# The end of an attention and maxout kernel: general-path transfers on GpSimd's queue, a last chunk of 384 and 128 columns, and a VectorE copy

## The chip, the cores and the metric

The kernel runs on one core of a Trainium2 chip. The metric is the device time of one execution in microseconds (us); a set of runs is given by its median. The profile is of one execution, and its times count from the first instruction of the program. Engines are TensorE (PE; PEld its weight loads), VectorE (DVE), ScalarE (ACT), GpSimd (POOL) and SyncE (SP). SyncE computes nothing here: it issues the DMA transfers and waits.

## The reference

For each of 8 batches and 8 heads, 512 tokens of width 64 attend to 32 state rows and the state rows attend to the tokens. The 512 + 32 rows of a batch, all heads side by side (512 columns), then pass a maxout layer.

```python
scores = scale * np.matmul(x, state.transpose(0, 1, 3, 2))     # softmax over the state rows
xread = np.matmul(a, state)
scores2 = scale * np.matmul(state, x.transpose(0, 1, 3, 2))    # softmax over the tokens
sread = np.matmul(a2, x)
x = concat([xread, sread], axis=2)  ->  (B * 544, 512)
h1 = x @ w1; h2 = x @ w2
out = np.maximum(h1, h2) @ w_out                               # float32, 4352 x 512
```

Softmax subtracts the maximum of each row first.

## The kernel before

The softmax is computed without subtracting a maximum, and the result is right as long as no sum of exponentials leaves a wide range. A flag is set where one does. Everything is computed by this fast path; then comes `tc.If(left_range >= 1, label="general")` at L658, whose body computes all batches again with the maximum subtracted. With the inputs here the flag is zero, the body is skipped, and every engine jumps over its own part of it. TensorE and ScalarE are given a hint at L631 that this jump is likely; VectorE, GpSimd and SyncE are not.

Maxout is rewritten as relu(x(w1 - w2)) w_out + x(w2 w_out). In the kernel `wd` is w1 - w2, `wo` is w_out and `wwo` is w2 w_out. For each batch, `SW[b]` holds the state times those two weights, `AT[b]` the transposed softmax weights, and `R[b]` the relu. `l1` computes `R`, and `l2(b, c)` computes a chunk `c` of 128 token rows by 512 columns: `l2_open` (2 matmuls at L384) opens the sum in a bank of the matmul memory, `l2_f` (8 matmuls at L389) adds the relu part, `l2_out` copies the bank into the batch's output tile `OB[b]`, and `store` (L405) sends it off. The state rows of all batches are done once at the end: `m1` (L418) and `m2(t)` (L426, L428), whose result goes out in four transfers of 64 KB each (L432). `copy` runs on ScalarE (L99), VectorE (L101) or GpSimd (L103).

Batches 0 and 1 run by an order written out by hand (`ORDER`), batches 2 to 6 in a loop, and batch 7 in a section of its own (L621 to L649). There the order is: `l1` of all 8 blocks, `m1`, the hints, the flag read into a register of every engine (L635), chunk 0 and both `m2` copied by VectorE, chunks 1 and 2 copied by ScalarE, and chunk 3 in two halves of 256 columns, each with its own bank, copied by ScalarE and stored by SyncE as soon as it is copied. The trailing copy at L653 waits for the store of chunk 2 to land, and a one-element matmul (L655) waits for that copy.

All transfers are issued from SyncE's queue, in program order, those of the general path too: two loads of `x` for each batch (L151), one store for each batch (L405) and eight of the state rows (L432). Completion is counted on eight DMA semaphores, taken in turn. For an engine or a semaphore that the general path would advance, the path that skips it has instructions that wait for the count so far and add what the body would have added (L658 in the profile). After that come closing waits on SyncE for every DMA semaphore and every engine's count, then a meeting of all engines, a clear of the program's semaphores by GpSimd, and a second meeting (all L740).

Of the kernel before, what the change touches and what calls it, by code (L numbers as in the profile page):

```python
# [48 lines left out]
def kernel(  # L49
# [9 lines left out]
    nc = tc.nc  # L59
    B, H, S, D = x.shape  # L60
    _, _, Ns, _ = state.shape
    L = S + Ns
# [25 lines left out]
    def bank(ring="r", dtype=F32):  # L88
        if isinstance(ring, int):
            i = ring  # L90
        else:
            r = rings[ring]
            i = r[turn[ring] % len(r)]
            turn[ring] += 1
        return banks[i] if dtype == F32 else banks[i].bitcast(BF16)

    def copy(eng, o, i):
        if eng == "A":
            nc.scalar.copy(o, i)  # L99
        elif eng == "V":  # L100
            nc.vector.tensor_copy(o, i)  # L101
        else:
            nc.gpsimd.tensor_copy(o, i)  # L103
# [36 lines left out]
    def h8(*shape):  # L140
        return stage.tile([128, *shape], F32, tag="h8", bufs=10, name="h8")
# [3 lines left out]
            wh[w, h] = h8(4, 512)  # L145
        return wh[w, h]

    def load_x(b, g):
        if b not in xf_t:
            xf_t[b] = h8(H, NC * D)  # L150
        nc.sync.dma_start(  # L151
            out=xf_t[b][:, 4 * g:4 * g + 4, :],
            in_=x[b, 4 * g:4 * g + 4].rearrange("h (p c) d -> p h (c d)", c=NC),
        )
# [53 lines left out]
    def d_(b):  # L208
        return st.setdefault(b, {})

    def cast_e(b, k, eng):
        d = d_(b)
        d["xe"] = xe[of_xe[b]]
        copy(eng, d["xe"][:, :, k, 8:136].rearrange("p c (j d) -> p j c d", j=2),
             xf_t[b][:, 2 * k:2 * k + 2, :].rearrange("p j (c d) -> p j c d", c=NC))
# [87 lines left out]
    def sr_mm(b, ring, nb=1):  # L303
        p = bank(ring)
        for j in range(nb):
            d = d_(b + j)
            for c in range(NC):
                for g in range(2):
                    for k in range(4):
                        o = 130 * j + 65 * g  # L310
                        nc.tensor.matmul(p[32 * k:32 * k + 32, o:o + 65], d["e"][:, g, c, k],  # L311
                                         d["xe"][:, c, k, 7 + 65 * g:72 + 65 * g],
                                         start=(j == 0 and c == 0 and g == 0),
                                         stop=(j == nb - 1 and c == NC - 1 and g == 1), skip_group_check=True)
        return p
# [9 lines left out]
    def sr_tr(b, ring, nb=1):  # L325
        p = bank(ring, BF16)
        for j in range(nb):
            nc.tensor.transpose(p[:, 128 * j:128 * j + 128], d_(b)["sr"][:, j].rearrange("p g d -> p (g d)"), ident)
        return p
# [52 lines left out]
    def l2_open(b, c, p, start, stop, lo=0, hi=DM):  # L382
        for g in range(2):
            nc.tensor.matmul(p[:, lo:hi], AT[b][:, g, c, :], SW[b][:, g, FF + lo:FF + hi],  # L384
                             start=(start and g == 0), stop=(stop and g == 1))

    def l2_f(b, c, p, fs, start, stop, lo=0, hi=DM):
        for j, f in enumerate(fs):
            nc.tensor.matmul(p[:, lo:hi], R[b][:, f, c * 128:(c + 1) * 128], wo[:, f, lo:hi],  # L389
                             start=(start and j == 0), stop=(stop and j == len(fs) - 1))  # L390

    def l2_out(b, c, p, eng, lo=0, hi=DM):
        if b not in OB:
            OB[b] = h8(NC, DM)
        copy(eng, OB[b][:, c, lo:hi], p[:, lo:hi])
# [7 lines left out]
    def store(b, c0=0, c1=NC, lo=0, hi=DM, eng=None):  # L403
        dst = out[b * L:b * L + S].rearrange("(p c) n -> p c n", c=NC)
        (eng or nc.sync).dma_start(out=dst[:, c0:c1, lo:hi], in_=OB[b][:, c0:c1, lo:hi])  # L405


    RS = {}
# [10 lines left out]
                                          start=(i == 0), stop=(i == 3))  # L419
        relu(RS["r"][:, f, :], p[:, 0:NT], eng)  # L420

    def m2(t, eng):
        p = bank("a")
        ts = slice(t * 128, (t + 1) * 128)
        for i in range(4):
            nc.tensor.matmul(p, sread_t[:, i, ts], wwo[:, i, :], start=(i == 0), stop=False)  # L426
        for f in range(NF):
            nc.tensor.matmul(p, RS["r"][:, f, ts], wo[:, f, :], start=False, stop=(f == NF - 1))  # L428
        copy(eng, RS["o"][:, t, :], p)
        for q in range(4):  # L430
            b = 4 * t + q
            nc.sync.dma_start(out=out[b * L + S:(b + 1) * L], in_=RS["o"][32 * q:32 * q + 32, t, :])  # L432


    def w2_cast(f, n, eng):
# [108 lines left out]
    for tok in toks:  # L544
        name, _, eng = tok.partition(">")
# [10 lines left out]
        elif w in mms:  # L556
            ring = [int(v) for v in ring]
            p = mms[w](*n, ring if w == "sw" else ring[0] if ring else None)
# [7 lines left out]
    for b in range(2, B - 1):  # L566
# [23 lines left out]
        if n in reads:  # L590
            p = sr_mm(*reads[n][:1], "a", reads[n][1])
# [18 lines left out]
        if n in reads:  # L610
            p = sr_tr(reads[n][0], "r", reads[n][1])
            sr_cp(p, reads[n][0], "A", reads[n][1])
        if n == B - 1:
            p = bank("r")
# [6 lines left out]
    b = B - 1  # L621
# [19 lines left out]
    store(b, 1, 2)  # L641
    l2(b, 2, "A")
    store(b, 2, 3)
    for lo, hi in ((0, 256), (256, 512)):
        p = bank("a")
        l2_open(b, 3, p, True, False, lo, hi)
        l2_f(b, 3, p, range(NF), False, True, lo, hi)
        l2_out(b, 3, p, "A", lo, hi)
        store(b, 3, 4, lo, hi)  # L649


# [2 lines left out]
    p = bank("a")  # L654
# [3 lines left out]
    with tc.If(left_range >= 1, label="general"):  # L658
        of_xe, of_e = [0, 1] * 4, [0, 1] * 4
        xf_t.clear(), st.clear(), AT.clear(), SW.clear(), R.clear(), OB.clear()  # L660
        mx = at.tile([128, 2 * NC, 2], F32, tag="mx", bufs=1, name="mx")
        cm = at.tile([64, 2], F32, tag="cm", bufs=1, name="cm")
        dl = h8(NC, DM)[:, 0, :]
        e2 = at.tile([64, 512], BF16, tag="e2", bufs=1, name="e2")
        for b in range(B):
            d = d_(b)
            for g in range(2):
                load_x(b, g)
            for k in range(4):
                cast_e(b, k, "PV"[k % 2])  # L670
            for hh in range(2):
                xt_ev(xt_mm(b, 2 * hh, 2, "r"), b, 2 * hh, 2, "V")
            for hh in range(2):
                pv = sc_mm(b, 2 * hh, 2).rearrange("p (c g i n) -> p g c i n", c=NC, g=2, i=2)
                for g in range(2):
                    m = mx[:, 4 * g:4 * g + 4]
                    dv = dl[:, 256 * g:256 * g + 256].rearrange("p (c i n) -> p c i n", c=NC, i=2)
                    nc.vector.tensor_reduce(m, pv[:, g], axis=AXX, op=ALU.max)
                    nc.vector.tensor_tensor(dv, pv[:, g], m.unsqueeze(3).to_broadcast([128, NC, 2, Ns]),
                                            op=ALU.subtract)  # L680
                nc.scalar.activation(out=e_view(b, 2 * hh, 2), in_=dl.rearrange("p (m i n) -> p m i n", i=2, n=Ns),
                                     func=ACTF.Exp, scale=scale)
                norm_sum(b, 2 * hh, 2)
                norm_mul(b, 2 * hh, 2, "V")
            for g in range(2):
                at_ev(at_mm(b, g, "r"), b, g, "V")
            for k in range(4):
                p = bank("r")
                for c in range(NC):
                    nc.tensor.matmul(p[0:64, c * 128:(c + 1) * 128], sbd[:, b, k, :], d["xt"][:, c, k, :],  # L690
                                     start=(c == 0), stop=(c == NC - 1))
                nc.vector.tensor_reduce(cm[:, 0:1], p[0:64], axis=AXX, op=ALU.max)
                nc.vector.tensor_scalar(cm[:, 1:2], cm[:, 0:1], scalar1=-scale, scalar2=None, op0=ALU.mult)
                nc.scalar.activation(out=e2, in_=p[0:64], func=ACTF.Exp, bias=cm[:, 1:2], scale=scale)
                pt = bank("r", BF16)
                for c in range(NC):
                    nc.tensor.transpose(pt[:, c * 64:(c + 1) * 64], e2[:, c * 128:(c + 1) * 128], ident[0:64, 0:64])
                copy("V", d["e"][:, :, :, k, :], pt[:, 0:256].rearrange("p (c g n) -> p g c n", c=NC, g=2))
            sr_ev(sr_mm(b, "r"), b)
            sr_cp(sr_tr(b, "r"), b, "V")  # L700
            for z in range(3):
                p = sw_mm(b, 512 * z, 512 * z + 512)
                for g in range(2):
                    sw_ev(p, b, 512 * z, 512 * z + 512, g, "V")
            for f in range(NF):
                l1(b, f, "V")
            for c in range(NC):
                l2(b, c, "V")
            store(b)
        m_open()  # L710
        for f in range(NF):
            m1(f, "V")
        for t in range(NT // 128):
            m2(t, "V")


# [28 lines left out]
```

## Time and profile before

| | |
|---|---|
| three runs | median 149.26 us, 148.87 to 149.98 |
| the profiled execution | 149.64 us, span from first to last instruction 147.8 us |
| mean granted TensorE clock | 0.994 |
| busy in the span | PE 140.6, DVE 79.6, ACT 67.7, POOL 52.9 us |
| DMA | 29.08 MB, mean 197 GB/s |

The span is what the page and the trace divide up; 1.8 us of the profiled execution lie around it. A busy TensorE is a matmul in flight, and matmuls overlap, so its share counts occupation. In the rows of groups the columns are the line, the engine, the operation, output and inputs, the shapes, the count, then busy time in us and the mean of one in ns, then the idle time ahead of them and what ended most of it. A row of one source line in the trace gives an engine (q for its instruction sequencer), the operation, the count, shortest/median/longest duration in ns, and the first and last start in us.

### The profile page before, as it was taken

Reading aid. Unit: us, or ns where it says so; the run is one execution under the profiler, and the core shown is the slowest. Engines: PE = TensorE matmul, PEld = TensorE weight load, DVE = VectorE, ACT = ScalarE, POOL = GpSimd, SP = SyncE. Lnnn points to the kernel's source line nnn. Section 1 sums busy time; section 2 is a strip of 40 time slices with the busy share of each in tenths; the row PEclk is TensorE's granted clock in tenths of the full one; section 3 lists DMA queues with packets and bytes.
Section 4 is the critical chain, followed back from the end, with each engine's and each line's share of the span. In section 5 each row is a group of like instructions: output and inputs, shape, how many; then the busy total and the mean of one; then the engine's idle time right before and its main releaser. Section 6 shows DMA issues by size and latency. Waiting matters only on the chain.

```text
span 147.8 us, 3126 instructions
## 1 busy us (share of the span) xinstructions
PE 140.6 (95%) x1254; PEld 68.8 (47%) x1254; DVE 79.6 (54%) x148; ACT 67.7 (46%) x130; POOL 52.9 (36%) x81
## 2 busy tenths in 40 slices
PE   6968999999999999999999999999999999999990
PEld 2534455445444445454534443454545344754460
DVE  3367754867599048463854575274637476632100
ACT  4367572677894236225632735270447145510121
POOL 3174315356996050924192447228300500000000
PEclk9999999999999999999999999999999999999997
DMA  4899999995786769495949698796306072002452
GB/s 146 249 379 361 363 362 246 338 349 190 137 301 133 186 231 305 88 263 191 279 80 306 246 124 158 266 315 115 75 29 255 0 212 112 35 0 82 104 180 78
DMA packets 35374, 29.08 MB, mean 197 GB/s; under 512 B 19900, under 2 KB 32444, under 8 KB 34588
## 3 DMA queue, kind: packets, MB, share of 16 engines
q1 hardware_dynamic: 35356, 28.84, 66.8%
q8 instruction: 11, 0.18, 0.5%
q14 instruction: 7, 0.06, 0.2%
HBM read 15.20 MB, written 8.91 MB: 163 GB/s over the span
## 4 chain that ended last, share of the span: by engine, by line
PE 70%; SPq 14%; DMA 10%; POOL 3%; issue 1%; ACT 1%; ACTq 0%
PE bank L389 32%; PE bank L371 16%; DMA h<-in_x_dram 8%; PE bank L384 8%; SPq L159 5%; SPq L163 4%; PE bank L344 4%; SPq L151 3%; PE bank L418 2%; PE bank L428 2%; PE bank L259 2%; PE bank L311 2%; SPq L192 2%; DMA out_dram<-h 1%; POOL xb L103 1%; PE bank L426 1%
## 5 line engine op out<-in xcount | busy, mean ns | idle before, releaser
L389 PE MATMUL bank<-wo,r 128*128 128x512 bf16 (+1 forms) x232 | 53.1, 372 | 0.0
L99 ACT COPY h<-bank 128x512 f32<-128x512 f32 (+1 forms) x20 | 11.1, 566 | 53.5 <-PE bank L389 49.0
L389 PEld LDWEIGHTS <-r 128*128 128x128 bf16 x232 | 22.7, 98 | 25.7
L371 PE MATMUL bank<-aT,sw 128*128 128x512 bf16 x128 | 29.8, 379 | 0.0
L362 DVE TENSOR_SCALAR r<-bank 128x512 bf16<-128x512 f32 x30 | 20.5, 690 | 13.9 <-PE bank L371 13.6
L360 ACT ACTIVATE r<-bank 128x512 bf16<-128x512 f32 x34 | 20.1, 598 | 7.4 <-PE bank L371 7.3
L277 POOL TENSOR_TENSOR a<-e,er 128x512 bf16<-128x512 bf16 (+1 forms) x13 | 12.3, 964 | 20.6 <-ACT e L267 16.4
L101 DVE CAST sw<-bank 128x512 bf16<-128x512 f32 (+1 forms) x23 | 13.7, 636 | 9.5 <-PE bank L344 9.4
L103 POOL CAST xb<-h 128x1024 bf16<-128x1024 f32 x12 | 12.4, 1039 | 17.6 <-issue 16.5
L371 PEld LDWEIGHTS <-sw 128*128 128x128 bf16 x128 | 12.0, 98 | 13.2 <-issue 0.2
L103 POOL CAST xe<-h 128x512 bf16<-128x512 f32 x24 | 14.4, 632 | 7.6 <-DMA h<-in_x_dram 7.6
L384 PE MATMUL bank<-sw,aT 128*128 128x512 bf16 (+1 forms) x58 | 16.9, 373 | 0.0
L99 ACT CAST sw<-bank 128x512 bf16<-128x512 f32 (+1 forms) x29 | 14.8, 572 | 1.6 <-PE bank L344 1.6
L101 DVE COPY h<-bank 128x512 f32<-128x512 f32 x13 | 8.7, 670 | 11.4 <-PE bank L389 11.3
L273 DVE TENSOR_REDUCE sums<-e 128x16 f32<-128x512 bf16 (+1 forms) x14 | 8.2, 586 | 1.7 <-ACT e L267 1.4
L463 PE MATMUL bank<-wo,w2t 128*128 128x512 bf16 x32 | 8.1, 379 | 0.5 <-ACT w2t L99 0.5
L516 PE MATMUL bank<-wo,r 128*128 128x512 bf16 x32 | 8.1, 379 | 0.0
L452 DVE TENSOR_TENSOR wd<-h,h 128x512 bf16<-128x512 f32 x7 | 5.8, 858 | 3.0 <-DMA h<-in_moe_w_dram 3.0
L471 PE MATMUL bank<-wz 128*128 128x512 bf16 x15 | 6.2, 565 | 1.2 <-DVE wz L474 1.2
L384 PEld LDWEIGHTS <-aT 128*128 128x128 bf16 x58 | 4.8, 98 | 5.2 <-issue 1.3
L267 ACT ACTIVATE e<-bank 128x512 bf16<-128x512 f32 (+1 forms) x14 | 6.8, 533 | 0.9 <-PE bank L259 0.4
L259 PEld LDWEIGHTS <-xt 128*128 128x128 bf16 x128 | 5.0, 98 | 2.6 <-DVE xt L101 0.6
(86 smaller groups left out, 122.8 us busy)
## 6 DMA issues: line engine op xcount, KB each, us to landing
h<-in_x_dram SPq DMA_DIRECT2D x16, 512.0 KB, 5.8
out_dram<-h SPq DMA_DIRECT2D x6, 1024.0 KB, 4.3
h<-in_moe_w_dram SPq DMA_DIRECT2D x8, 512.0 KB, 9.2
h<-in_moe_w_out_dram SPq DMA_DIRECT2D x4, 512.0 KB, 9.1
out_dram<-h SPq DMA_DIRECT2D x2, 512.0 KB, 3.7
out_dram<-h SPq DMA_DIRECT2D x3, 256.0 KB, 2.2
out_dram<-rs SPq DMA_DIRECT2D x8, 64.0 KB, 2.3
sf<-in_state_dram SPq DMA_DIRECT2D x2, 224.0 KB
```

The lines of the kernel that those rows point to most:

```text
L99: nc.scalar.copy(o, i)
L101: nc.vector.tensor_copy(o, i)
L103: nc.gpsimd.tensor_copy(o, i)
L273: nc.vector.tensor_reduce(s_, e_view(b, k0, kn), axis=AXX, op=ALU.add)
L277: (nc.gpsimd if eng == "P" else nc.vector).tensor_mul(e_view(b, k0, kn, "a"), e_view(b, k0, kn), d_(b)["er"][:, :, k0:k0 + kn].unsqueeze(3 ...
L360: recent["A"] = nc.scalar.activation(out=o, in_=p, func=ACTF.Relu)
L362: nc.vector.tensor_scalar(o, p, scalar1=0.0, scalar2=None, op0=ALU.max)
L371: nc.tensor.matmul(p, SW[b][:, g, f * 128:(f + 1) * 128], AT[b][:, g].rearrange("p c t -> p (c t)"), start=(g == 0), stop=(g == 1))
L384: nc.tensor.matmul(p[:, lo:hi], AT[b][:, g, c, :], SW[b][:, g, FF + lo:FF + hi], start=(start and g == 0), stop=(stop and g == 1))
L389: nc.tensor.matmul(p[:, lo:hi], R[b][:, f, c * 128:(c + 1) * 128], wo[:, f, lo:hi], start=(start and j == 0), stop=(stop and j == len(fs) ...
L463: nc.tensor.matmul(ACC[key], w2t[:, j, i, :], wo[:, j, :], start=first(key), stop=last(key, j == f + n - 1))
L516: nc.tensor.matmul(p, R[b][:, j, c * 128:(c + 1) * 128], wo[:, j, :], start=first(key), stop=last(key, j == f + n - 1))
```

## The change

Three edits. `load_x` and `m2` take an engine to issue from, and the general path passes `nc.gpsimd` to them and to `store`. So all 32 transfers of the general path move from SyncE's queue to GpSimd's; the fast path's transfers stay where they are. The last chunk of batch 7 is split at column 384 in place of 256, and its second part, now 128 columns, is copied by VectorE; ScalarE copies the first.

```diff
-    def load_x(b, g):
+    def load_x(b, g, eng=None):
         if b not in xf_t:
             xf_t[b] = h8(H, NC * D)
-        nc.sync.dma_start(
+        (eng or nc.sync).dma_start(
...
-    def m2(t, eng):
+    def m2(t, eng, dma=None):
...
-            nc.sync.dma_start(out=out[b * L + S:(b + 1) * L], in_=RS["o"][32 * q:32 * q + 32, t, :])
+            (dma or nc.sync).dma_start(out=out[b * L + S:(b + 1) * L], in_=RS["o"][32 * q:32 * q + 32, t, :])
...
-    for lo, hi in ((0, 256), (256, 512)):
+    for lo, hi, eng in ((0, 384, "A"), (384, 512, "V")):
         p = bank("a")
         l2_open(b, 3, p, True, False, lo, hi)
         l2_f(b, 3, p, range(NF), False, True, lo, hi)
-        l2_out(b, 3, p, "A", lo, hi)
+        l2_out(b, 3, p, eng, lo, hi)
         store(b, 3, 4, lo, hi)
...
             for g in range(2):
-                load_x(b, g)
+                load_x(b, g, nc.gpsimd)
...
-            store(b)
+            store(b, eng=nc.gpsimd)
...
         for t in range(NT // 128):
-            m2(t, "V")
+            m2(t, "V", nc.gpsimd)
```

In the program this makes, the order on each engine is the same up to the last chunk. TensorE then has ten matmuls of 384 and ten of 128 columns where it had twenty of 256; ScalarE has one copy fewer and VectorE one more, directly ahead of its branch at L658. In the part that skips the general path, SyncE's eight instructions on DMA semaphores are gone, and GpSimd has four waits and one instruction for eight new semaphores of its own queue. SyncE's closing waits are twelve instead of eight, each naming up to two semaphores: the four first name the new ones, the next eight are the old ones, in the old order and with the same engine counts beside them.

## The prediction

> **What bounds the kernel now.** I read the page's busy times and its chain of waits first.
>
> ```profile
> PE 140.6 (95%) x1254; PEld 68.8 (47%) x1254; DVE 79.6 (54%) x148; ACT 67.7 (46%) x130; POOL 52.9 (36%) x81
> ...
> PE 70%; SPq 14%; DMA 10%; POOL 3%; issue 1%; ACT 1%; ACTq 0%
> ```
>
> TensorE bounds the body: 140.6 us of a 147.8 us span, and most of the chain. The change leaves the body alone. The order of the instructions shows no difference on any engine before the last chunk of batch 7, so everything up to 141.7 us should stand. What can move are the 6 us from there to the span's end, so next I read the timeline of the end.
>
> ```profile
> 141.75 0.38 PE L384 MATMUL bank<-sw,aT 128*128 128x256 bf16 x2
> ...
> 143.04 0.37 ACT L99 COPY h<-bank 128x256 f32<-128x256 f32 x1 [0.51 <-PE bank L389]
> 143.06 1.04 PE L389 MATMUL bank<-wo,r 128*128 128x256 bf16 x8
> 144.13 0.37 ACT L99 COPY h<-bank 128x256 f32<-128x256 f32 x1 [0.72 <-PE bank L389]
> 144.68 0.19 ACT L653 CAST h<-wz 128x1 f32<-128x1 bf16 x1 [0.17 <-DMA out_dram<-h]
> 144.92 0.09 PEld L655 LDWEIGHTS bank<-h 128*1 128x1 f32 x2 [1.11 <-ACT h L653]
> ```
>
> The last matmul's result is free at 144.11, ScalarE copies it until 144.50, SyncE issues the last store at 144.53 and it lands at 146.44 (the last two are from the trace's DMA records). No engine computes after 145.2, and yet the span runs to 147.83. Third, therefore, the branch around the general path (L658) and the closing waits (L740), SyncE's in the stretch behind 146 us.
>
> ```profile
> L658 SPq EVENT_SEMAPHORE  x8: 17/17/17, 145.1 to 146.5; - x8
> L658 POOLq COMPARE_BRANCH  x1: 45/45/45, 124.1 to 124.1; - x1
> L658 POOLq EVENT_SEMAPHORE  x1: 17/17/17, 124.3 to 124.3; - x1
> L658 DVEq COMPARE_BRANCH  x1: 72/72/72, 137.7 to 137.7; - x1
> L658 DVEq EVENT_SEMAPHORE  x1: 21/21/21, 140.8 to 140.8; - x1
> L658 ACTq COMPARE_BRANCH  x1: 68/68/68, 144.7 to 144.7; - x1
> L658 SPq COMPARE_BRANCH  x1: 45/45/45, 144.9 to 144.9; - x1
> ```
> ```profile
> L740 SPq EVENT_SEMAPHORE  x8: 28/28/28, 146.5 to 147.0; - x8
> L740 SPq DRAIN  x2: 7/10/13, 147.0 to 147.1; - x2
> ```
>
> Two things are to be seen. (a) SyncE, on the path that skips the general block, makes up for that block's DMAs: eight instructions that wait for one DMA semaphore each and add to it. Seven are through by 145.6; the eighth waits for the last landing and goes at 146.46. Only then come eight more waits (L740), 62 ns apart, then two drains and the meeting of all engines: 146.46 to 147.83 is 1.37 us. (b) From VectorE's branch to its next instruction 3.08 us pass (137.72 to 140.80), against 0.18 to 0.19 on GpSimd (124.09 to 124.27) and SyncE (144.91 to 145.10). The copy before that branch was done at 138.39, so it explains at most 0.7 of the 3.08. VectorE's part of the general path is some 430 instructions long and that jump has no prefetch hint; TensorE's and ScalarE's have one (L631). Now this stall costs nothing: VectorE is through by 140.9, six microseconds early.
>
> **The change, part by part.**
>
> *SyncE's part of the general path.* Its 32 DMAs go to GpSimd's program. In the program that the change makes, SyncE's skip block is empty, and its closing waits are twelve: four for the GpSimd queue's new semaphores, then the old eight, each of them asking for less. All but the last can pass before the last store lands. What lay behind the landing, 146.46 to 147.10 (second drain), shrinks to the last wait and two drains: from the last L740 wait at 146.965 to the end are 0.87 us where the landing had 1.37. Worth -0.50, provided that SyncE waits for nothing else.
>
> *GpSimd.* Its skip block gains four waits on semaphores that ask for zero and one instruction that adds to the eight new semaphores. It takes its branch at 124.1, 23 us before it is needed; by the row of the same instruction at the span's start (27 ns) and GpSimd's closing steps of under 0.2 us this is about 0.5 us, or 3.6 if its longer block made it stall as VectorE does. Nothing in either case. If that cover were gone, it would be 0.5 to 3.6 on the end. The 32 transfers themselves are not executed, since the flag is zero.
>
> *The closing clear* takes 25 semaphores instead of 17. The row has 135 ns for 17; between no change and in proportion (+64 ns) I take +0.03.
>
> *384 and 128 columns.* TensorE issues ten matmuls of 512 columns every 216 ns and of 256 every 109 ns, which makes 0.416 ns a column and 2.6 ns apiece (64-column ones at L259 come every 29 ns, as this has it). Ten of 384 and ten of 128 give 10 x (162.5 + 55.9) = 2.18 us, as before: the end of TensorE stays at 144.11. The 384 columns are free at about 143.55 instead of 143.02. ScalarE's copy of them costs 0.48 (a 128x384 copy took 485 ns), to 144.05 (a wait that it gets ahead of it asks for a VectorE copy done at 133.1), and its store is issued at 144.08 instead of 143.44.
>
> *The last 128 columns on VectorE.* It has been idle since 138.4 and its copy is not queued behind anything. Rows near it: 420 ns for 256 columns, 682 for 512, hence 290 for 128 (an operation on 128x128 from the same memory took 291). 144.13 to 144.42, where ScalarE ended at 144.50. But SyncE is in the issue of the 384 columns until 144.41, and 0.09 lies between one issue and the next (143.77 to 143.81, then 47 ns as at 140.47): the last store goes at 144.51 instead of 144.53. It is 64 KB behind 192 KB, where now 128 KB follow 128 KB. Landing after issue was 1.92 for the last one; 64 KB stores of L432 show 1.6 to 3.4, median 2.3. I take 1.92, as the nearest in place: 146.42, bounds 146.1 to 146.8 (by 2.3). So by this route alone the end would come at 146.42 + 0.02 + 0.87 = 147.3, which is -0.53, +0.03 for the clear.
>
> *The branch behind that copy.* A step that the words of the change don't name, and the one that decides. VectorE's branch is in order behind its last copy. That was dispatched at 137.70, with the branch 23 ns later; now it is dispatched at 144.13, the branch at 144.15. With the 3.08 us of its own row, its next instruction, which adds to VectorE's semaphore, comes at 147.23 and is seen at 147.26. Queued behind it is VectorE's drain for the meeting (0.12 later); and SyncE waits for it, because its closing wait for the third-last store asks for VectorE's full count too. SyncE arrives there at about 145.7 and stands until 147.28. It passed the same wait at 146.844, and 0.99 us follow (two waits, two drains, the meeting, the clear). The landing at 146.4 is hidden under this.
>
> *Sum.* 147.28 - 146.84 = +0.43, +0.03 for the clear: +0.46 us. On the profiled execution: span 147.83 to 148.29, time 149.64 to 150.10 (1.81 lie around the span). That execution is 0.38 over the median of the three runs, 149.26, so I forecast 149.26 + 0.46 = 149.7.
>
> [...]
>
> Bounds of the stall: instruction-queue packets of 8 KB took 0.31 to 0.84 us, the one nearest behind VectorE's branch (138.75) 0.54. With the shortest the stall is 2.85, with the longest 3.4, and if another engine's packet (0.55 at 145.76) goes ahead of it, 3.9. Together 149.5 to 150.5 for this case.
>
> **The rivals.**
>
> *Faster: VectorE's stall is short in its new place.* If VectorE idles for six microseconds ahead of the branch, and something fetches its target meanwhile, it costs what SyncE's does (0.19), VectorE is through by 144.5, and the last store binds: 149.26 - 0.53 + 0.03 = 148.8. It turns at a stall of 3.08 - 0.46 = 2.62 us: under this the change is faster. For it: ScalarE's branch cost 0.48 with a hint long before it, so an early fetch works. Against it: VectorE was idle ahead of its branch before as well (1.97 us before the copy at 137.70), and still took 3.08. [...]
>
> *Longer stall.* The last stores (145.2 to 145.9) and the pages that SyncE, ScalarE and TensorE fetch when they branch (144.7 to 144.9) now share the queues with VectorE's fetch. One page of 1.3 us as at 146.06 ahead of it: 149.7 + 1.3 = 151.0. Against it: the stretch 137.7 to 140.8 was no lighter, the DMA engines busy 39% of it, against 30% in 144.1 to 147.2.
>
> *The GpSimd queue costs something outside the skip block.* A program that uses this queue may need more around the span, where 1.81 us lie now; doubled, 149.7 + 1.8 = 151.5. Nothing in the order of the instructions shows it: the start is the same in both, down to an instruction on that queue's semaphores at 0.14 us.
>
> **How the numbers follow.** A measurement of this kernel tells about 1%, 1.5 us, from no change. Forecast 0.60 (0.57 within 1%, 0.03 slower); faster rival 0.20 (0.16 within, 0.04 faster, should the landing come early as well); longer stall 0.12 (0.05 within, 0.07 slower); queue 0.08 (0.02 within, 0.05 slower, 0.01 faster). So faster 0.05, same 0.80, slower 0.15. The range goes from 148.5, the faster rival with an early landing, to 150.8, the forecast's upper bound and the runs' own spread of some 0.3; the likeliest case's own range is 149.5 to 150.5.
>
> **What would show it.** In the profile after: SyncE with no L658 instruction but its branch; twelve L740 waits, a stop ahead of the tenth; VectorE's copy of 128x128 at 144.1 and its L658 semaphore instruction near 147.2; last landing near 146.4; span 148.3. I am wrong if VectorE's next instruction follows its branch in under 2.6 us, if anything differs before 141.7, or if the time around the span leaves 1.8 us.

## The result, and the profile after

| | median | runs |
|---|---|---|
| before | 150.03 us (148.85 to 151.26) | 22 |
| after | 150.55 us (149.53 to 152.33) | 22 |

The ratio is 1.0054, with a 95% interval of 1.0028 to 1.0081: the change makes the kernel slower by about 0.8 us (0.4 to 1.2). The ratio leaves out executions over 1.5% above their kernel's fastest, so the 152.33, which is the execution of the page after; the medians of all runs lie 0.52 us apart. The forecast was slower by 0.46, to 149.7. Of the 0.85 us from there to 150.55, 0.77 lie in the starting point: three runs put before at 149.26, 22 runs at 150.03.

The spans of two single profiles don't show this. In the profile after, the last chunk of batch 7 begins at 143.46 us where it began at 141.75, although the program up to there is the same; a second profile of the changed kernel has 141.60, and in the ten profiles of the other kernels below it is 140.87 to 142.26. That difference is there by 38 us of the span, arises with the first weight loads (median landing 10.8 us after issue on the page after, 9.2 before) and is no part of the change. So all profiles are compared by their **tail**: from the last chunk's first matmul (0.21 us behind its weight load) to the span's end; "in the tail" below counts from that matmul. It is 6.09 us before, 6.97 after, and 6.88 in the second profile of the same kernel: +0.79 to +0.88, which agrees with the measured slowdown.

The page after, busy times and chain of waits:

```profile
PE 139.7 (93%) x1236; PEld 68.6 (46%) x1254; DVE 80.3 (53%) x149; ACT 67.4 (45%) x129; POOL 53.6 (36%) x81
...
PE 75%; DMA 9%; SPq 9%; DVE 2%; issue 1%; ACT 1%; DVEq 0%; ACTq 0%
```

The body is as it was (18 matmul records are missing, by 1254 weight loads), with one copy moved from ScalarE to VectorE. VectorE's sequencer (DVEq) is in the chain now, with a share that rounds to nothing.

The branch around the general path, after, in the trace's rows of line L658 (engine, operation, count, shortest/median/longest ns, first and last start in us):

```profile
L658 DVEq COMPARE_BRANCH  x1: 72/72/72, 145.9 to 145.9; - x1
L658 ACTq COMPARE_BRANCH  x1: 68/68/68, 146.4 to 146.4; - x1
...
L658 SPq COMPARE_BRANCH  x1: 50/50/50, 146.6 to 146.6; - x1
L658 ACTq EVENT_SEMAPHORE  x1: 17/17/17, 146.9 to 146.9; - x1
...
L658 DVEq EVENT_SEMAPHORE  x1: 21/21/21, 149.3 to 149.3; - x1
```

VectorE branches before any other engine but GpSimd, and has its next instruction last: 3.49 us later (145.858 to 149.348). SyncE has no semaphore instruction at L658 any more. Its closing waits, and what the longest of them waited for (from the waits on SyncE's queue: us in total, times, longest):

```profile
L740 SPq EVENT_SEMAPHORE  x14: 17/28/1981, 146.8 to 150.4; - x14
```
```profile
SPq L740 <- DVEq L658: 2.0, 1, 2.0
```

Fourteen are the twelve closing waits and two of the meeting. One of them stands for 1981 ns, and it is the one that asks for VectorE's count. The timeline of the end of the chunk:

```profile
145.28 0.48 ACT L99 COPY h<-bank 128x384 f32<-128x384 f32 x1 [1.04 <-PE bank L389]
145.84 0.29 DVE L101 COPY h<-bank 128x128 f32<-128x128 f32 x1 [5.74 <-PE bank L389]
146.38 0.19 ACT L653 CAST h<-wz 128x1 f32<-128x1 bf16 x1 [0.61 <-DMA out_dram<-h]
```

Subtract 1.71 to lay this beside before: the copies are where the prediction had them, 143.57 and 144.13, with 0.48 and 0.29 us. What it did not have is in the trace's DMA records: the last store, issued 0.03 us *earlier* in the tail than before (2.75 against 2.78), lands 2.86 us after its issue, not 1.92, and the store of the 384 columns 3.07 us after, where the last but one took 1.85. The records also have packets of the kind instruction, in the tail 8 KB on q14 and 16 KB on q8. They are called instruction packets, or pages, below; the records give their queue, not the engine that they are for.

### The profile page after: what moved, and what is told of

Same layout as the page of the kernel before. It is cut to its first block, busy times and chain, and to the rows that moved or that the text cites. A ratio compares the mean times of both kernels' runs of the same rounds, so it can differ in the third digit from the quotient of the medians.

```text
span 150.4 us, 3110 instructions
## 1 busy us (share of the span) xinstructions
PE 139.7 (93%) x1236; PEld 68.6 (46%) x1254; DVE 80.3 (53%) x149; ACT 67.4 (45%) x129; POOL 53.6 (36%) x81
## 4 chain that ended last, share of the span: by engine, by line
PE 75%; DMA 9%; SPq 9%; DVE 2%; issue 1%; ACT 1%; DVEq 0%; ACTq 0%
PE bank L389 31%; PE bank L371 17%; DMA h<-in_moe_w_dram 8%; PE bank L384 8%; PE bank L344 4%; SPq L159 4%; SPq L163 4%; PE bank L516 3%; PE bank L418 2%; PE bank L428 2%; PE bank L259 2%; PE bank L311 2%; DMA out_dram<-h 1%; PE bank L522 1%; DVE wd L452 1%
## 5 line engine op out<-in xcount | busy, mean ns | idle before, releaser
L389 PE MATMUL bank<-wo,r 128*128 128x512 bf16 (+2 forms) x227 | 52.6, 371 | 0.4
L277 POOL TENSOR_TENSOR a<-e,er 128x512 bf16<-128x512 bf16 (+1 forms) x13 | 11.8, 923 | 23.2 <-ACT e L267 18.9
L101 DVE COPY h<-bank 128x512 f32<-128x512 f32 (+1 forms) x14 | 9.0, 643 | 17.2 <-PE bank L389 17.0
L103 POOL CAST xe<-h 128x512 bf16<-128x512 f32 x24 | 14.9, 653 | 4.4 <-DMA h<-in_x_dram 4.4
L384 PE MATMUL bank<-sw,aT 128*128 128x512 bf16 (+2 forms) x51 | 15.4, 372 | 0.2
L344 PE MATMUL bank<-wd,sbd 64*32 64x512 bf16 (+1 forms) x144 | 5.9, 358 | 1.3 <-DVE wd L452 1.3
## 6 DMA issues: line engine op xcount, KB each, us to landing
h<-in_moe_w_dram SPq DMA_DIRECT2D x8, 512.0 KB, 10.8
```

The lines of the kernel that those rows point to most:

```text
L277: (nc.gpsimd if eng == "P" else nc.vector).tensor_mul(e_view(b, k0, kn, "a"), e_view(b, k0, kn), d_(b)["er"][:, :, k0:k0 + kn].unsqueeze(3 ...
L344: nc.tensor.matmul(pg[g][32 * i:32 * i + 32, 0:n], sbd[64 * g:64 * g + 64, b, i, 32 * g:32 * g + 32], rhs, start=True, stop=True)
```

## The experiments

All in one table first; times from the profiles, in us. "Stall" is from VectorE's branch to its next instruction, in brackets where the branch lies ahead of the last chunk; "landing" is of the last store, after its issue; "sets the end" is what SyncE's last long wait was for.

| kernel | tail | stall | landing | sets the end | ratio to before, 95% |
|---|---|---|---|---|---|
| before | 6.09 | (3.08) | 1.92 | landing, then 1.37 of SyncE | |
| after; again | 6.97; 6.88 | 3.49; 3.40 | 2.86; 2.75 | VectorE's count | 1.0054; 1.0064 (1.0024 to 1.0105) |
| queue only | 5.68 | (2.98) | 1.95 | landing | 0.9961 (0.9924 to 0.9997) |
| split and VectorE only | 6.93 | 3.42 | 2.78 | landing | 1.0024 (0.9986 to 1.0062) |
| after + hint | 7.05 | 3.56 | 2.92 | VectorE's count | 1.0051 (1.0017 to 1.0085) |
| after, short general path | 6.24 | 0.60 | 2.55 | landing | 1.0008 (0.9972 to 1.0044) |
| queue, split, both on ScalarE; again | 5.48; 5.49 | (2.89; 2.85) | 1.77; 1.77 | landing | 0.9963 (0.9920 to 1.0007); 0.9976 (0.9933 to 1.0018) |
| after in halves | 6.40 | 2.92 | 2.11 | VectorE's count | 0.9990 (0.9955 to 1.0026) |
| queue, split, both on ScalarE, pages later | 6.25 | (2.87) | 1.75 | TensorE's count | one run |
| queue only, no trailing copy | 6.15 | (3.01) | 2.41 | landing | 1.0022 (0.9978 to 1.0066) |
| after, engines exchanged | 6.07 | 3.15 | 2.22 | VectorE's count | 0.9973 (0.9932 to 1.0014) |

Most ratios have an interval of some 0.4% to each side, 0.6 us, about as wide as the effects. The tails repeat to 0.1 us, and the verdicts rest on them.

**The queue alone.** The three edits to the general path's transfers as in the change; the last chunk as before.

```diff
-    for lo, hi, eng in ((0, 384, "A"), (384, 512, "V")):
+    for lo, hi in ((0, 256), (256, 512)):
...
-        l2_out(b, 3, p, eng, lo, hi)
+        l2_out(b, 3, p, "A", lo, hi)
```

> Only the general path's transfers move to GpSimd's queue; the last chunk stays in 256 and 256 columns, both copied by ScalarE. The tail is the time from the last chunk's first matmul to the span's end: 6.08 us before, 6.94 after. Theory (VectorE's branch stall is the whole loss): VectorE is through early again, SyncE waits for the last landing only, tail about 5.6, ratio to before 0.9965. Rival Q (the GpSimd queue and the longer closing waits cost): tail 6.5 or more, ratio 1.003 or more. Rival S (the split and the smaller last store cost): the same as the theory here, told apart by the next kernel.

5.68 and 0.9961. Its SyncE waits at the end for the landing alone:

```profile
SPq L740 <- DMA out_dram<-h: 0.7, 1, 0.7
```

So the queue is a gain of 0.40 us, and rival Q, that it costs, is out.

**The split and VectorE alone.** Before, with only the last chunk's part of the diff.

> Only the last chunk's part of the change: 384 and 128 columns, the second copied by VectorE; all transfers stay on SyncE's queue. Theory: VectorE's branch stalls for 3.1 to 3.5 us behind its copy, SyncE stops at its closing wait for VectorE's count, and SyncE's eight skip instructions, which come first, are hidden under that stop: tail 6.5 to 6.9, ratio 1.003 to 1.006, about that of the whole change. Rival Q: nothing of its kind is in here, so ratio 1.000 or a little under. Rival S: last landing over 0.4 us later than before and the end 1.37 us behind it.

The tail (6.93) was at the upper end of the range; the reason was another. The rows at L658 and SyncE's waits:

```profile
L658 SPq EVENT_SEMAPHORE  x8: 17/17/17, 145.6 to 147.8; - x8
L658 DVEq COMPARE_BRANCH  x1: 72/72/72, 144.7 to 144.7; - x1
...
L658 DVEq EVENT_SEMAPHORE  x1: 21/21/21, 148.1 to 148.1; - x1
```
```profile
SPq L658 <- SPq L658: 1.9, 3, 1.6
```

SyncE's eighth skip instruction waited for the last landing, until 147.8 (5.54 in the tail, where before had 4.70), and 1.37 us of SyncE's own followed as before. When it came to the wait for VectorE's count, VectorE had just got there. So rival S had something: the last store did land 0.84 later. Two losses lay side by side, and neither shows in the other's presence.

**A hint for VectorE's branch.**

```diff
-    engs = [mybir.EngineType.PE, mybir.EngineType.Activation]
+    engs = [mybir.EngineType.PE, mybir.EngineType.Activation, mybir.EngineType.DVE]
```

(and the hint placed behind VectorE's last relu, 14 us ahead of the branch; lines below move down by one)

> The whole change, with a prefetch hint for VectorE's branch as TensorE and ScalarE have it. Theory: VectorE's next instruction comes about 0.5 us after its branch instead of 3.49, the last landing binds, tail about 5.55, ratio to before 0.996. Rival Q: the tail stays above 6.5. Rival N (the stall has nothing to do with fetching, VectorE simply takes 3 us to branch): stall unchanged, ratio 1.005.

The hint did nothing on VectorE, while TensorE, which jumps over 3073 instructions with a hint, goes on after 0.55 us as it did before:

```profile
L659 DVEq COMPARE_BRANCH  x1: 90/90/90, 143.7 to 143.7; - x1
...
L659 PEldq COMPARE_BRANCH  x1: 489/489/489, 144.4 to 144.4; - x1
...
L659 PEldq EVENT_SEMAPHORE  x1: 51/51/51, 145.0 to 145.0; - x1
L659 DVEq EVENT_SEMAPHORE  x1: 21/21/21, 147.2 to 147.2; - x1
```

By itself this spoke for rival N. The trace's DMA records show that the hint brought no page early: between it and the branch one 8 KB instruction packet begins, 7.0 us ahead of the last chunk, and the change without the hint has the same one there. Why the hint fails here stays open.

**A short general path.** The whole change, with the body's `for b in range(B)` as `range(1)`.

> The whole change, no hint, but the general path (skipped here) is written for batch 0 alone, which leaves the other seven batches out of it: VectorE's part of it is 81 instructions long instead of 510. Theory (what counts is how far VectorE jumps): stall falls to 0.2 to 0.5 us, tail about 5.55, ratio 0.996. Rival N: stall still 3 us or more, tail 6.5 to 6.9, ratio 1.005.

```profile
L658 DVEq COMPARE_BRANCH  x1: 72/72/72, 143.8 to 143.8; - x1
...
L658 DVEq EVENT_SEMAPHORE  x1: 21/21/21, 144.4 to 144.4; - x1
```
```profile
SPq L740 <- DMA out_dram<-h: 1.3, 2, 0.7
```

With 81 instructions to jump over in place of 510, VectorE goes on after 0.60 us, in the first 0.28 of which its own copy is still running. This settles rival N: distance makes VectorE's stall here, 0.60 us over 81 instructions and 3.40 to 3.49 over 510. But the tail was 6.24 and not 5.55, because the last store still took 2.55 to land. So the stall was not the whole loss, and the question became what makes the last store late.

**The split with both copies on ScalarE.**

```diff
-    for lo, hi, eng in ((0, 384, "A"), (384, 512, "V")):
+    for lo, hi, eng in ((0, 384, "A"), (384, 512, "A")):
```

> The whole change, but ScalarE copies the last 128 columns too; VectorE is through early. Theory now (two limits side by side: VectorE's stall of 3.5 us, and a last store that lands 2.9 us after its issue instead of 1.9, because its data now run into the instruction pages that are fetched after the branches): the landing alone is left, 2.3 to 2.6 us after the issue with VectorE's page out of the way, tail 6.1 to 6.4 us. Rival V (VectorE's stall is the whole loss): landing 1.9, tail 5.7, as with the queue alone.

Too pessimistic: 5.48, the shortest tail of all, and a landing of 1.77.

```profile
SPq L740 <- DMA out_dram<-h: 0.4, 1, 0.4
```

The stores have the same sizes and the same issue times as in the change (2.33 and 2.75 in both). So 64 KB behind 192 KB is not slow, and the split gains 0.20 over the queue alone. The figures are those of rival V, or better. That the stall is nevertheless not the whole loss rests on the short general path, where the stall was 0.60 and the landing still late. It is the VectorE copy that makes the stores late (2.86 and 2.75 with it, 1.77 without), in a second way beside the stall: with it two 8 KB instruction packets begin 3.9 to 4.2 us into the tail, over the short path too (3.93 and 3.98), and without it one (4.00).

**Halves, the second on VectorE.**

```diff
-    for lo, hi, eng in ((0, 384, "A"), (384, 512, "V")):
+    for lo, hi, eng in ((0, 256, "A"), (256, 512, "V")):
```

> The whole change with two halves of 256 columns in place of 384 and 128; VectorE copies the second half. Theory: the stall is 3.1 to 3.6 us, SyncE stops at the wait for VectorE's count, tail 6.6 to 7.0; the last landing is 2.0 to 2.3 us after its issue (its data end before the pages come) and doesn't bind. Rival W (the stall is long because the late stores are in its way): stall back to 3.0.

```profile
L658 DVEq COMPARE_BRANCH  x1: 72/72/72, 143.8 to 143.8; - x1
...
L658 DVEq EVENT_SEMAPHORE  x1: 21/21/21, 146.8 to 146.8; - x1
```

The stall is 2.92, rival W's figure, and VectorE's count still sets the end: 6.40, below the range I gave. VectorE branches at the same point of the tail (2.40). But here the data of the last but one store are over at 3.05, and an instruction packet begins at 3.43, between the two stores and 1.03 us after the branch, as before; in the change the 384 columns' data run from 3.16 to 4.00 and the packets begin at 4.00 and 4.20, 1.60 us or more after the branch.

**Pages later.** The trailing copy at L653 (and L655) on `OB[b][:, 3, 0:1]` in place of `OB[b][:, 2, 0:1]`, on the kernel with both copies on ScalarE.

> As the split with both copies on ScalarE, but the trailing copy, and with it ScalarE's and TensorE's branches, waits for the store of the 384 columns to land instead of chunk 2's, so their instruction pages are fetched later. Theory: the last two landings come 1.9 to 2.1 us after their issue, as before the change, and no page packet overlaps their data. Rival D (64 KB in pieces of 512 B behind 192 KB is slow by itself): last landing still 2.3 us or more.

Landing 1.75 against 1.77: in that kernel the pages behind the branches of ScalarE and TensorE had not been in the way, and rival D is out. The later branches of these two now set the end instead, 6.25:

```profile
SPq L740 <- PEq L658: 1.3, 1, 1.3
```

**No trailing copy.** The queue part alone, with the lines of L653 to L655 taken out.

> The queue part alone (256 and 256 columns on ScalarE), without the trailing copy and one-element matmul at L653 and L655, so ScalarE and TensorE branch some 0.5 us earlier and their pages are fetched during the last store's data. Theory: that store lands 2.3 us or more after its issue instead of 1.95, tail 6.0 to 6.4 instead of 5.7. Rival D: landing stays 1.9 to 2.0, tail 5.7.

As the theory had it: ScalarE branches 0.55 us earlier, TensorE even 2.93, and instruction packets come at 2.72 and 3.50 instead of 4.00 and 4.31, among the stores' data, and the last two landings take 3.20 and 2.41 instead of 1.85 and 1.95. Here the stores are unchanged and VectorE is not involved; only the time of the branches moved.

**Engines exchanged.**

```diff
-    for lo, hi, eng in ((0, 384, "A"), (384, 512, "V")):
+    for lo, hi, eng in ((0, 384, "V"), (384, 512, "A")):
```

> The whole change with the engines exchanged: VectorE copies the 384 columns, ScalarE the last 128. Theory (VectorE's branch time plus its stall sets the end, and its page must come ahead of the last stores' data): the branch comes 0.57 us earlier, at 1.83 us after the last chunk's first matmul, the stall is 2.9 us as where no store is in the way, SyncE passes the wait for VectorE's count at about 4.8 where the change had 5.94, tail 5.8, last landing under 2.2 us after issue. Rival (any VectorE copy in the last chunk costs the same, whenever it comes): tail 6.9.

Branch at 1.84, stall 3.15, SyncE past the wait at 5.04, tail 6.07. The rival (6.9) is out; the stall was 0.25 longer than I gave it, the tail 0.27. One packet begins at 3.16, just ahead of the data of the first store (3.24), but 1.32 us after the branch, although no data packet runs from 2.50 on. So this extra 0.25 is not explained.

**The best version and the change, timed again.** Both on one chip, in turn.

> Queue and split, both copies on ScalarE, timed again beside the change itself. Tail 5.5 us as before, ratio to before 0.995 to 0.997.

> The change itself, timed again on the same chip: tail 7.0 us, stall 3.4 to 3.6, ratio to before 1.005.

The tails repeat, 5.49 and 6.88. Against the change the kernel with both copies on ScalarE is faster (149.92 and 150.27 us median there; the intervals of their ratios to before do not touch: 0.9933 to 1.0018 and 1.0024 to 1.0105). Against before its tail is 0.6 us shorter in both profiles, which would be 0.4%; its two ratios are 0.37% and 0.24% under 1, and each interval just includes 1. So it beats the change by the ratios, and before by the tails alone.

## Why the prediction was right or wrong

The mechanism was right, step by step: the queue removes SyncE's work behind the last landing (0.40 us); VectorE's branch, in order behind its new copy, stalls (3.49); SyncE stops at the wait for VectorE's count (1.98). The size was wrong, and so the call: +0.46 us was put within the 1%, 1.5 us, that a measurement was taken to tell, and it is +0.8 and told, as 22 runs have an interval of 0.4 us to each side. One sign of being wrong did appear, a difference before 141.7; it lies in the weight loads' times and not in the program.

- *SyncE's part*: -0.50, clear +0.03. Measured with the queue alone: -0.40, the clear's row 178 ns for 135 (+0.04). Right.
- *The split*: no change on TensorE, last issue 0.02 earlier. Measured 0.03. With "by this route alone" -0.53 + 0.03, the kernel without VectorE's copy has -0.60. Right, a little cautious: the landing is 1.77, not 1.92.
- *The branch behind the copy*: this is the step that failed, by the term of the stall. I took 3.08 from before's row, and bounded it by 2.85 to 3.9. It is 3.49 (3.40 in the second profile): SyncE passes at 5.94, where 5.53 was forecast, and that 0.41 is the whole miss of the sum. Where the branch lies ahead of the last chunk, the stall is 2.85 to 3.08, in six profiles; the four with a VectorE copy of the last 128 columns over a long jump have 3.40 to 3.56. The rival "longer stall" was thus the mechanism at a third of its price. Before's row was taken at a time with a similar total of DMA traffic (39% busy against 30%), and I argued from that total. By my estimate from these profiles, what counts is what is in flight about one microsecond after the branch: the first packet that can be VectorE's begins 1.03 us behind its branch before and in halves, and 1.52 to 1.60 in those four, about when the 384 columns' data end. The engines exchanged (1.32) fit this only in part. That the stall contains one 8 KB packet, as the bounds have it, was my estimate from the packet behind before's branch; no run shows it apart. What the runs show is 0.60 over 81 instructions and 3.40 to 3.49 over 510. The length of the jump, "some 430" instructions, is 504 before and 510 after.
- *The landing*: taken at 1.92 with bounds of 1.6 to 2.3, measured 2.86, outside them. It didn't set the end only because the stall was worse. Without the stall the tail would be about 6.55 by estimate (the landing is at 5.61 in the tail, and 0.94 follow the landing with the short general path), still above 6.09. That is also where the forecast's stall would have put the end, so that the landing stayed hidden, as forecast, was luck. I had VectorE's stall lengthened by the stores, but not the stores' landings by instruction packets.
- *Faster rival*, a short stall: out. The branch takes 72 to 90 ns on VectorE, and over the long path the next instruction comes 2.85 to 3.56 us later. What spoke for an early fetch, ScalarE's 0.48, was weak evidence: its part is 85 instructions long, about as short as the 81 that cost VectorE 0.60 without a hint.
- *Queue rival*: out, by the queue alone; around the span lie 1.9 us on the page after and 1.8 in the second profile.
- *GpSimd at no cost*: right, though its skip took 1.1 us (125.80 to 126.89) where 0.5 was taken; it was over 22 us early.

From before to after: queue -0.40, split -0.20 (both shown by a kernel each), VectorE's copy +1.49 (5.48 to 6.97). Of that last, the stall and the late landing overlap, so they don't add up. That the landing is late because of instruction packets near the stores is shown in direction by the kernel without the trailing copy and by the two with and without VectorE's copy; how 8 KB packets of 0.31 and 0.80 us delay a landing by 1.1 is not shown: the data end 0.6 us later (4.69 in the tail, against 4.06 with both copies on ScalarE), and the landing follows 0.92 behind them instead of 0.47. The DMA records narrow it. In these records each store has sixteen counts on its semaphore, and its landing is given here by the last. Of the change's last store fifteen counts come by 4.67 and one at 5.61, of the 384 columns' fifteen by 4.27 and one at 5.40; with both copies on ScalarE all sixteen come by 4.53 and by 4.35. So a single count of each store is late, and not the whole store.

## What to carry to other kernels

An engine that must jump over a long block at the end of a kernel (VectorE's 510 instructions here took 3.40 to 3.56 us behind its copy of the last 128 columns, 81 took 0.60) should do its last work early; before giving the last copy to an idle engine, look at what stands behind that copy in its program, and time it from its own branch row. Make the last wait the only thing behind the last landing: each closing wait of SyncE there cost its 62 ns in full. And price a stall by what will be in flight at its new place, in both directions: here it went from 3.08 to 3.49 us, and the last landing from 1.92 to 2.86.

## What was not expected of the hardware

In these profiles VectorE's stall over the long path is 3.40 to 3.56 us behind a copy of the last 128 columns, 2.92 behind one of the last 256, and 2.85 to 3.08 with its branch ahead of the last chunk. The landings differ with the branches too: the last store takes 1.75 to 1.95 us to land where VectorE has branched long before and ScalarE and TensorE branch after its issue, and 2.1 to 2.9 where VectorE's branch, or an early one of those two, comes ahead of it; the store before it takes up to 3.2. A prefetch hint had no effect on VectorE's branch (3.56 us with it, 3.49 and 3.40 without), in a program where TensorE's hinted one takes 0.55. And the last of 192 KB and 64 KB, issued 0.42 us apart, lands sooner after its issue (1.77) than the last of two of 128 KB 1.09 us apart (1.92 to 1.95).
